# One order over two pairs of steps for each block of nine output products

## The chip, the cores and the metric

The kernel runs on one core of a Trainium2 chip. The metric is device microseconds of one execution. Three runs of the kernel before gave 1625.9, 1626.43 and 1627.45 us; the median, 1626.43, is the time before. The profile is one further execution of 1627.72 us, whose span (first to last instruction of the program) is 1625.8 us.

## The reference

One input `x` (2048 tokens, 512 channels) is normalized and goes through two branches: attention with 32 heads of 16 columns, and an MLP over the token axis (a mixer) with 1792 hidden units.

```python
xn = _layernorm(x)
q, k, v = split_heads(xn @ wqkv)                       # 32 heads of 16
p = softmax(einsum("bhqd,bhkd->bhqk", q, k) * 16**-0.5)
s = merge_heads(einsum("bhqk,bhkd->bhqd", p, v)) @ wo
h = _layernorm(xn)
u = gelu(einsum("bsd,sf->bdf", h, w1) + b1)
y = einsum("bdf,fs->bds", u, w2) + b2
out = x + s * silu(transpose(y))
```

## The kernel before, in words

Heads are worked on two at a time (NP = 16 pairs of heads). For a pair of heads the 2048 x 2048 scores are computed twice: once to find the largest score of each query, and once more, with that maximum subtracted by two extra rows of the operands, for the exponentials. The work is cut into 512 steps, NT = NU = 512, 32 for each pair of heads.

- `max_of` (line 523) issues one matmul into a bank of the ring `ps_mx` (three PSUM banks; line 532) and a VectorE reduction of that bank (line 536). Below, a **maximum** (m).
- `score` (line 980) issues one matmul into a bank of the ring `ps_sc` (four banks; line 987) and a ScalarE exponential that reads it (line 992). Below, a **score** (s). Scores run 22 steps (LEAD) behind the maxima.
- `values` (line 994) multiplies one step's exponentials with the values (line 1003) on all 128 rows of TensorE, two further steps later.

A maximum or a score needs at most 50 of TensorE's rows, so two matmuls run side by side, one on rows 0 to 63 and one on rows 64 to 127. Such a place for two is called a **slot** here. Products of the rest of the network fill the places that the attention leaves free: each of their matmuls over 128 rows is cut into two halves over 64 rows (`halves`, line 1132; the matmul is line 1144). These halves are the letter **D**. First comes the mixer (`mixer`, line 573), then the product with `wo` (`rest`, line 1011): a block of 128 tokens takes nine products, three for each of the first three groups of eight heads, and fourteen blocks (PARTS) are done this way while the maxima still run (steps below NU).

The products of a block add up in one bank, which `Banks.hold` takes out of the front of the ring `ps_sc` when the block's first product is fetched (line 1034), so that the scores go round on three banks. A ScalarE copy in `part` (line 910) empties the bank, and it goes to the end of the ring.

The main loop (line 1227) goes by pairs of steps, s and s+1. A pair has eight maxima, eight scores, two `values` and some D. How many D is set by `count` (line 1155): a block of nine is given out as 4 and 5. The order inside a pair is written out by hand:

```python
4: ("DDDDssmmsmms", "smsmmmssDDDD", 4, 7),
5: ("DDDDDsmsmsmsm", "smsmsmsmDDDDD", 5, 8),
```

The two strings are the two row halves, one letter a slot. The two numbers are places: ahead of the slot with that number stand `values` of one step and `run_later`, and at the first of the two places also `piece`. The half that begins with D changes from pair to pair (`lead`). `values` uses all the rows, so it parts the slots into groups. For a block of nine (a pair with 4 and one with 5) these are: a **three-slot group** (slots 4 to 6 of the first pair), a **ten-slot group** (slots 7 to 11 and the next pair's 0 to 4; nine D), a three-slot group (slots 5 to 7), and a **nine-slot group** (slots 8 to 12 and the next block's first four; nine D, of two blocks).

Other engines' work is issued at those places:

- `run_later` (line 514) runs functions put off with `after(n, f)`, n places later: the copy of the values' sum (`put_away`, line 716), ScalarE's casts of the divided attention (`parts`, line 792, instruction on line 798), the mixer's last identity (line 703, issued at the end of a mixer block) and tanh (line 704), GpSimd's additions, stores.
- `piece` (line 1220) issues one short VectorE job: the two parts of `max_rows` (line 538), once for 16 steps (first a reduction on line 551 and one 32x32 transpose on line 548; later three transposes, GpSimd's cast and subtraction, and four DMAs that put the maxima into the operand rows), or a reciprocal (line 751).
- At the start of each pair the loop calls `divisions` and `load_second`, which issue loads on SP.

Of the kernel before, what the change touches and what calls it, by code (L numbers as in the profile page):

```python
# [21 lines left out]
def tile_attention_token_mixer(ctx, tc, x, wqkv, wo, w1, b1, w2, b2, out):  # L22
    nc = tc.nc
    P = 128
    S, D = x.shape
# [11 lines left out]
    LEAD = 22  # L37
# [132 lines left out]
    with (  # L170
# [97 lines left out]
        def first(c, some=range(4), power=False):  # L268
            def dst(b):
                xn[4 * c + b] = px.tile([P, D], F32, name="xn", bufs=8)  # L270
                return xn[4 * c + b]

            return Norm(lambda b: xr[4 * c + b], dst, some=some, power=power)
# [69 lines left out]
        two = first(0, range(2, 4), True)  # L343
# [64 lines left out]
        for c in range(NC):  # L408
# [20 lines left out]
            for n, (part, g) in enumerate(order):  # L429
                m = slice(g * P, (g + 1) * P)  # L430
# [75 lines left out]
    now = [0]  # L506

    def after(n, f):

        later.append(f if n == 1 else lambda: after(n - 1, f))  # L510
# [3 lines left out]
    def run_later():  # L514
        now, later[:] = soon + later, []
        soon.clear()
        for f in now:
            f()

    NU = NP * NB * 2  # L520
# [406 lines left out]
    def load_second():  # L927

        b = next((b for b in unkept if b >= PARTS), min(unkept))
        unkept.remove(b)  # L930
        i = b - NB // 2
        while not held or len(held) < NB // 8:
            held.append(big.tile([P, S], F32, name="big"))
        ys[b] = held[i // 4][:, i % 4 * 512 : i % 4 * 512 + 512]
        nc.sync.dma_start(ys[b], y_d[b] if b < PARTS else xv[:, b, :])
# [58 lines left out]
    def values(t):  # L994
        p, r = divmod(t, SPP)
        span, kb = divmod(r, NB)
        if kb == 0:
            state["av"] = ps_av.tile([P, 512], F32, name="av")
        av = state["av"]
        for a in range(2):  # L1000
            for c in range(2):
                j = 2 * a + c
                nc.tensor.matmul(  # L1003
                    av[32 * j : 32 * j + 32, :],
                    vps[p][:, kb, 16 * a : 16 * a + 32], prob.pop((t, a, c)),
                    start=kb == 0, stop=kb == NB - 1,
                )
        if kb == NB - 1:
            soon.append(lambda: put_away(p, span, av))
# [46 lines left out]
    class Fill:  # L1056
# [10 lines left out]
        def next(self):  # L1067
            x = self.peek()
            self.ahead.clear()
            return x  # L1070
# [3 lines left out]
    done = 0  # L1074
    n_fill = NF * 3 * NB + NB * 3 * NF
    total = NT + LEAD
# [4 lines left out]
    def take(n, each):  # L1081

        nonlocal open_, done
        got = 0
        while open_ and (got < n or fill.peek() and len(fill.peek()) == 2):
            x = fill.next()
            if x is False:
                open_ = False
            elif x is None:
                break  # L1090
            elif len(x) == 2:
                def then(empty, back):
                    empty()
                    back()

                each(None, lambda x=x: then(*x))
                if fill.peek() is None:
                    fill.next()
                    break
            else:  # L1100
                each(x, None)
                got += 1
        done += got
# [28 lines left out]
    def halves(lead, n):  # L1132


        parts, then = ([], []), []

        def each(x, f):
            if f:
                then.append(f)
                return  # L1140
            ps, w, m, first, last = x
            for a, made in ((lead, parts[0]), (1 - lead, parts[1])):
                r = slice(64 * a, 64 * a + 64)
                made.append(lambda r=r, start=first and a == lead, stop=last and a != lead: nc.tensor.matmul(  # L1144
                    ps, w(r), m(r), start=start, stop=stop,
                ))

        take(n, each)
        return *parts, then
# [3 lines left out]
    new_block = [False]  # L1153

    def count():


        left = -done
        for i, n in enumerate(sizes):
            left += n  # L1160
            if left > 0:
                break
        new_block[0] = left == n
        if left == 9:
            return 4
        return min(6, -(-left // -(-3 * left // (15 if i == SLOW else 16)))) if left > 0 else 0
# [35 lines left out]
    def items(s, a):  # L1202

        mx, sc = [], []
        for i in range(4):
            t = s - LEAD + i // 2
            if s < NU:
                mx.append(lambda i=i: max_of(s + i // 2, i % 2, a))
            if 0 <= t < NT:
                sc.append(lambda t=t, i=i, at=(ps_mx, "mx") if a and s >= NU else (ps_sc, "sc"): score(t, i % 2, a, *at))  # L1210
        return mx, sc

    take(FIRST, whole)
    after(5, lambda: load_v(0))
    if NP > 1:
# [4 lines left out]
    def piece():  # L1220
        if pieces:
            pieces.pop(0)()
            return True
        return False

    lead = 0
    for s in range(0, total + 1, 2):
        t = s - LEAD
        now[0] = s
        if s >= NU or t < 0:  # L1230
            run_later()
        if done >= n_fill // 2 + 3 * NF:
            divisions()
        if s >= NU - SPP + LEAD and unkept:
            load_second()
        if s == NU:

            ps_sc.free += ps_mx.free
            ps_mx.free = ps_sc.free
        heads = [items(s, a) for a in range(2)]  # L1240
        if s < NU and t >= 0:
            steady[0] = True
            one, two, then = halves(lead, count())
            made = [dict(D=part, m=heads[a][0], s=heads[a][1]) for part, a in ((one, lead), (two, 1 - lead))]
            first, second, *places = order(len(one), new_block[0])
            if one:
                lead = 1 - lead
            for i, kinds in enumerate((*zip(first, second), "")):
                if i in places:

                    if i == places[0]:
                        piece()
                    now[0] = s + places.index(i)
                    if now[0] >= LEAD + 2:
                        values(now[0] - LEAD - 2)
                    run_later()
                for of, kind in zip(made, kinds):
                    if of[kind]:
                        of[kind].pop(0)()
            for f in then:  # L1260
                f()
        elif s < NU:

            for i in range(4):
                for a in range(2):
                    max_of(s + i // 2, i % 2, a, *first_banks[n_max % 4])
                    n_max += 1
                end = i == 3 and s + 2 == LEAD
                some = []
                take(EARLY[n_max // 2 % len(EARLY)], lambda *x: some.append(x))  # L1270
                for x in some:
                    lanes(*x, stop=end and x is some[-1])
                if end:
                    keep_half()
                if i == 1:
                    now[0] = s + 1
                    run_later()
        else:


            for i in range(2):

                a_half(*(heads[a][1][2 * i : 2 * i + 2] for a in range(2)), i == 0 or s >= NU + 2 * (PARTS - NB // 2))
                if not piece() and asides and s < total - 2:
                    asides.pop(0)()
                for v in range(t - 2, t + i):
                    if (v, 0, 0) in prob:
                        values(v)
                if i == 0:
                    now[0] = s + 1  # L1290
                    run_later()
            if s == NU + 4:
                load_last_w()
            for _ in in_halves[:2]:
                load_half()
            if s == total - 6:
                split_last_w()
        if s < NU and s % 16 == 14:
            pieces[:0] = max_rows(s + 1)
        while t < 0 and piece():  # L1300
            pass
        for v in (t - 2, t - 1):
            if 0 <= v < NT and (v, 0, 0) in prob:
                values(v)
        if 0 <= t < NT:
            p, r = divmod(t, SPP)
            if r == 0 and p + 1 < NP:
                if p > 0:
                    load_qk(p + 1)
                load_v(p + 1)  # L1310
# [23 lines left out]
    one, two, times, lower = asides  # L1334
# [5 lines left out]
    of = ks[NP - 1][:, :1024].rearrange("p (a q) -> p a q", a=2)  # L1340
# [81 lines left out]
```

## Time and profile before

| | before |
|---|---|
| median of three runs | 1626.43 us |
| the profiled execution | 1627.72 us |
| its span | 1625.8 us |
| TensorE matmul (PE) busy | 1618.6 us, 11937 instructions |
| VectorE (DVE) busy | 1421.3 us, 2492 |
| ScalarE (ACT) busy | 1195.8 us, 2312 |
| maxima, reductions on line 536 | 2026, 682 ns each in the record |
| scores, exponentials on line 992 | 2004, 607 ns each |
| products of `wo` during the maxima, line 1144 | 252 half products, 1402.4 to 1556.4 us |

Times in a row are microseconds from the start of the span. A row of the timeline gives the start, the length, the engine, the line, the operation and what it writes and reads; "x8" merges eight instructions that follow each other on that engine, with the length from the first one's start to the last one's end. PEld is the loading of a matmul's weights. In brackets stands the idle time of the engine ahead of the row and what ended it. A matmul's record is longer than the time until the next may start, so starts are compared, not lengths.

### The profile page before, as it was taken

Reading aid. Unit: us, or ns where it says so; the run is one execution under the profiler, and the core shown is the slowest. Engines: PE = TensorE matmul, PEld = TensorE weight load, DVE = VectorE, ACT = ScalarE, POOL = GpSimd, SP = SyncE. Lnnn points to the kernel's source line nnn. Section 1 sums busy time; section 2 is a strip of 40 time slices with the busy share of each in tenths; the row PEclk is TensorE's granted clock in tenths of the full one; section 3 lists DMA queues with packets and bytes.
Section 4 is the critical chain, followed back from the end, with each engine's and each line's share of the span. In section 5 each row is a group of like instructions: output and inputs, shape, how many; then the busy total and the mean of one; then the engine's idle time right before and its main releaser. Section 6 shows DMA issues by size and latency. Waiting matters only on the chain.

```text
span 1625.8 us, 31245 instructions
## 1 busy us (share of the span) xinstructions
PE 1618.6 (100%) x11937; PEld 876.6 (54%) x11937; DVE 1421.3 (87%) x2492; ACT 1195.8 (74%) x2312; POOL 559.9 (34%) x665
## 2 busy tenths in 40 slices
PE   9999999999999999999999999999999999999998
PEld 7888854554555544544545545545545445444444
DVE  7665999999999999999999999999999999999956
ACT  3333477777777777778877877777777778888885
POOL 1224844342244432342333332322322233632440
PEclk9999999999999999999999999999999999999999
DMA  7478441514142141926151512314151615353365
GB/s 228 177 249 206 114 93 41 95 43 73 41 71 71 32 79 34 244 66 109 39 86 38 86 61 44 76 25 69 38 85 38 112 39 94 120 98 119 115 186 194
DMA packets 152466, 155.60 MB, mean 96 GB/s; under 512 B 51628, under 2 KB 110252, under 8 KB 149244
## 3 DMA queue, kind: packets, MB, share of 16 engines
q1 hardware_dynamic: 147900, 152.85, 38.6%
q8 instruction: 94, 1.54, 0.4%
q0 software_dynamic: 4416, 0.75, 0.4%
q14 instruction: 56, 0.46, 0.1%
HBM read 101.86 MB, written 50.58 MB: 94 GB/s over the span
## 4 chain that ended last, share of the span: by engine, by line
PE 99%; DMA 0%; DVE 0%; ACT 0%; SPq 0%; issue 0%; POOL 0%; DVEq 0%
PE av L1003 31%; PE dn L1144 24%; PE sc L987 16%; PE mx L532 15%; PE sc L435 3%; PE dn L670 3%; PE mx L435 2%; PE av L435 1%; PE sc L101 0%; PE sc L103 0%; PE sc L102 0%; PE mx L987 0%; DMA wl<-in_A_wqkv_dram 0%; PE mx L101 0%; PE mx L103 0%; PE mx L102 0%
## 5 line engine op out<-in xcount | busy, mean ns | idle before, releaser
L536 DVE TENSOR_REDUCE mxp<-mx 128x1 f32<-128x512 f32 x2026 | 1251.8, 682 | 118.3 <-PE mx L532 100.3
L992 ACT ACTIVATE prob<-sc 128x512 f32<-128x512 f32 x2004 | 1039.3, 607 | 284.6 <-PE mx L532 126.8
L532 PE MATMUL mx<-big 48*128 48x512 f32 x2026 | 773.7, 419 | 0.0
L987 PE MATMUL sc<-big 50*128 50x512 f32 x2004 | 739.8, 412 | 0.1
L1003 PE MATMUL av<-prob,vp 128*32 128x512 f32 x4096 | 545.5, 604 | 0.2 <-DVE ev L721 0.2
L1144 PE MATMUL dn<-hu,wh 64*128 64x512 f32 x1520 | 507.4, 404 | 0.0
L987 PEld LDWEIGHTS sc<-big 50*128 50x128 f32 x2004 | 354.2, 186 | 238.8 <-ACT prob L992 210.6
L532 PEld LDWEIGHTS mx<-big 48*128 48x128 f32 x2026 | 358.0, 185 | 195.4 <-DVE mxp L536 178.2
L1144 PEld LDWEIGHTS dn<-hu,wh 64*128 64x128 f32 x1520 | 271.9, 184 | 73.6 <-issue 49.5
L1144 PE MATMUL dn<-hu,wl 64*128 64x512 f32 x762 | 302.3, 397 | 0.0
L1003 PEld LDWEIGHTS av<-prob,vp 128*32 128x32 f32 x4096 | 80.9, 108 | 180.3 <-issue 168.0
L94 POOL TENSOR_TENSOR wl<-raw,wh 128x512 fp32r<-128x512 f32 x124 | 150.7, 1217 | 60.0 <-ACT wh L166 26.6
L1144 PEld LDWEIGHTS dn<-hu,wl 64*128 64x128 f32 x762 | 140.5, 184 | 12.1
L164 POOL CAST wh<-raw 128x512 fp32r<-128x512 f32 x104 | 60.4, 580 | 192.1 <-PE mx L532 79.5
L559 POOL CAST m<-f 16x128 fp32r<-16x128 f32 x32 | 9.0, 280 | 303.6 <-DVE f L548 303.6
L98 POOL DMA_DIRECT2D big<-m x128 | 66.2, 525 | 2.7 <-PE mx L987 2.7
L620 POOL TENSOR_TENSOR sq<-u 128x512 f32<-128x512 f32 x11 | 11.4, 1041 | 133.0 <-ACT u L614 132.9
L1144 PE MATMUL dn<-wh,hu 64*128 64x512 f32 x168 | 55.1, 393 | 0.0
L707 POOL TENSOR_SCALAR t<-t 128x512 f32<-128x512 f32 x16 | 23.8, 1488 | 83.7 <-ACT t L704 83.7
L435 PE MATMUL sc<-xt,big 128*128 128x512 f32 x184 | 44.3, 389 | 0.0
L94 POOL TENSOR_TENSOR hu<-hx,hu 128x512 fp32r<-128x512 f32 x16 | 20.4, 1292 | 68.4 <-ACT hu L278 68.4
L670 PE MATMUL dn<-hu,wh 64*128 64x512 f32 x128 | 42.3, 392 | 0.0
(233 smaller groups left out, 1212.1 us busy)
## 6 DMA issues: line engine op xcount, KB each, us to landing
raw<-in_B_w_dram SPq DMA_DIRECT2D x104, 256.0 KB
big<-k_d SPq DMA_DIRECT2D x96, 128.0 KB
big<-q_d SPq DMA_DIRECT2D x96, 128.0 KB
q_d<-sg SPq DMA_DIRECT2D x16, 512.0 KB
k_d<-sg SPq DMA_DIRECT2D x16, 512.0 KB
num_d<-ev SPq DMA_DIRECT2D x30, 256.0 KB
u_d<-uo SPq DMA_DIRECT2D x14, 512.0 KB
hu<-u_d SPq DMA_DIRECT2D x14, 512.0 KB
```

What stands on the lines that cost most here:

```text
L94: eng.tensor_tensor(out=o, in0=a, in1=b.bitcast(F32), op=OP.subtract)
L98: queue.dma_start(dst.bitcast(F32), src.bitcast(F32))
L164: nc.gpsimd.tensor_copy(whs[n][:, :m, :], raws[n][:, :m, :])
L435: nc.tensor.matmul(ps, w[part][:, kd, m], xt[kd][:, z, :], start=w is wh and z == 0 and kd == 0, stop=w is wl and kd == ND - 1,)
L532: nc.tensor.matmul(ps, q[o : o + 48, r * P : (r + 1) * P], k[o : o + 48, c * 512 : (c + 1) * 512], start=True, stop=True,)
L536: nc.vector.tensor_reduce(mxp[u // 16][:, a, r % 8, c : c + 1], ps, axis=AX.X, op=OP.max)
L670: nc.tensor.matmul(ps, w(slice(0, 64)), m(slice(0, 64)), start=first, stop=last)
L707: nc.gpsimd.tensor_scalar(t, t, 1.0, None, op0=OP.add)
L987: nc.tensor.matmul(ps, ks[p][o : o + 50, kb * P : (kb + 1) * P], qs[p][o : o + 50, at : at + 512], start=True, stop=True,)
L992: nc.scalar.activation(e, ps, AF.Exp, scale=scale)
L1003: nc.tensor.matmul(av[32 * j : 32 * j + 32, :], vps[p][:, kb, 16 * a : 16 * a + 32], prob.pop((t, a, c)), start=kb == 0, stop=kb == NB - 1,)
L1144: made.append(lambda r=r, start=first and a == lead, stop=last and a != lead: nc.tensor.matmul(ps, w(r), m(r), start=start, stop=stop,))
```

## The change: one order of 25 slots for a block

While the blocks of nine run, the loop takes two pairs of steps together. `both_pairs` has an order of 25 slots, with `values` and `run_later` ahead of slots 2, 12, 15 and 24. The nine D of the first half stand in slots 3 to 11, those of the other half in slots 15 to 23. The nine products are fetched, and with them the bank, at slot 3; the copy that empties it is issued behind slot 23. `piece` is called ahead of slots 2 and 15. The groups between `values` are now: slots 2 to 11 (ten slots), 12 to 14 (three), 15 to 23 (nine) and 24 with the next block's 0 and 1 (three). `divisions` and `load_second` of the second pair are called ahead of slot 15. The order is used where s divides by 4, the mixer is done, and a new block of nine is due; the second pair is then passed over.

```diff
+    WIDE = ("mssDDDDDDDDDsmsmsmmssmsmm", "smmsmsmsmsmsmmsDDDDDDDDDs", 2, 12, 15, 24)
+
+    def both_pairs(s, keep):
+
+        heads = [[x + y for x, y in zip(items(s, a), items(s + 2, a))] for a in (lead, 1 - lead)]
+        made = [dict(m=mx, s=sc) for mx, sc in heads]
+        first, second, *places = WIDE
+        one, two, then = [], [], []
+        for i, kinds in enumerate((*zip(first, second), "")):
+            if i in places:
+                n = places.index(i)
+                if n == 2:
+                    keep(s + 2)
+                if n % 2 == 0:
+                    piece()
+                now[0] = s + n
+                values(now[0] - LEAD - 2)
+                run_later()
+            if "D" in kinds and not one and not two:
+                one, two, then = halves(lead, 9)
+                assert len(one) == len(two) == 9
+            for of, rows, kind in zip(made, (one, two), kinds):
+                (rows if kind == "D" else of[kind]).pop(0)()
+            if then and not two:
+                then.pop()()
...
     lead = 0
-    for s in range(0, total + 1, 2):
-        t = s - LEAD
-        now[0] = s
-        if s >= NU or t < 0:
-            run_later()
+    second_pair = None
+
+    def keep(s):
+
         if done >= n_fill // 2 + 3 * NF:
             divisions()
         if s >= NU - SPP + LEAD and unkept:
             load_second()
+
+    for s in range(0, total + 1, 2):
+        t = s - LEAD
+        now[0] = max(s, now[0])
+        if s >= NU or t < 0:
+            run_later()
+        if s != second_pair:
+            keep(s)
...
         heads = [items(s, a) for a in range(2)]
-        if s < NU and t >= 0:
+        if s == second_pair:
+            pass
+        elif s < NU - 2 and s % 4 == 0 and done >= n_fill and count() == 4 and new_block[0]:
+            both_pairs(s, keep)
+            second_pair = s + 2
+        elif s < NU and t >= 0:
```

## The prediction

> **What bounds the kernel now.** First the page: the span, each engine's share of it, the granted clock, and the chain that ended last.
>
> ```profile
> span 1625.8 us, 31245 instructions
> ...
> PE 1618.6 (100%) x11937; PEld 876.6 (54%) x11937; DVE 1421.3 (87%) x2492; ACT 1195.8 (74%) x2312; POOL 559.9 (34%) x665
> ...
> PEclk9999999999999999999999999999999999999999
> ...
> PE 99%; DMA 0%; DVE 0%; ACT 0%; SPq 0%; issue 0%; POOL 0%; DVEq 0%
> ```
>
> TensorE sets the end at full clock, so only time taken from or put onto its stream counts. A busy TensorE may still be waiting (a blocked matmul isn't shown as idle), so second I look for the place: the lines of the changed stage, from the view by source line.
>
> ```profile
> L1144 PE MATMUL dn<-wh,hu x168: 383/391/490, 1402.4 to 1556.4; 64*128 64x512 f32 x168
> L910 ACT COPY t<-dn x14: 592/593/595, 1414.2 to 1557.1; 128x512 f32<-128x512 f32 x14
> ```
>
> The D products of the output blocks run from 1402.4 to 1556.4, up to the last pair of steps with maxima (s=510). Fourteen blocks of two pairs are 56 steps, so the first has s=456: it divides by 4, and the new branch takes all fourteen. One block lasts (1557.1-1414.2)/13 = 10.99 us.
>
> Third, what a block would last unhindered, from the timeline of the mixer, where a pair has 5 D:
>
> ```profile
> 1304.40 1.07 PE L1003 MATMUL av<-prob,vp 128*32 128x512 f32 x8
> ...
> 1305.40 0.49 PE L987 MATMUL sc<-big 50*128 50x512 f32 x1
> ...
> 1306.30 1.07 PE L1003 MATMUL av<-prob,vp 128*32 128x512 f32 x8
> ...
> 1309.85 1.06 PE L1003 MATMUL av<-prob,vp 128*32 128x512 f32 x8
> ```
>
> A pair of 13 slots takes 5.45 us. `values` with its changeover takes 1.00 (1304.40 to the slot at 1305.40), the three-slot group 0.90, the ten-slot group 3.55-1.00 = 2.55. So a slot costs (2.55-0.90)/7, about 0.23. A block has 25 slots, one fewer than two such pairs: 2 x 5.45 - 0.23 = 10.67. The stage loses 0.32 us per block. Where? The timeline of a nine-slot group:
>
> ```profile
> 1456.45 0.49 PE L532 MATMUL mx<-big 48*128 48x512 f32 x1
> ...
> 1456.78 0.40 PE L987 MATMUL sc<-big 50*128 50x512 f32 x1
> ...
> 1457.21 1.09 ACT L992 ACTIVATE prob<-sc 128x512 f32<-128x512 f32 x2 [0.56 <-PE dn L1144]
> ...
> 1457.87 0.18 PEld L987 LDWEIGHTS sc<-big 50*128 50x128 f32 x1 [0.19 <-ACT prob L992]
> ...
> 1458.18 0.59 ACT L910 COPY t<-dn 128x512 f32<-128x512 f32 x1
> ...
> 1458.20 0.40 PE L532 MATMUL mx<-big 48*128 48x512 f32 x1
> ...
> 1459.01 1.07 PE L1003 MATMUL av<-prob,vp 128*32 128x512 f32 x8
> ```
>
> It lasts 2.56 us against 2.55-0.23 = 2.32. The new block has just taken a bank out of the ring, so the score at 1457.87 must use the bank of the score at 1456.78, two scores back: its exponential runs 1457.21 to 1457.81, and the bank is free 0.06 later. The wait is 0.15 (due 1457.72, after the five slots' 0.33 + 4 x 0.23), and the next slot comes 0.33 after instead of 0.23. From here on slot k of a group (from 0) is due at 0.33 + 0.23 x (k-1), `values` 0.37 after the last; an exponential or a reduction starts 0.43 after its matmul, as at 1456.78, and 0.54 after the first of a group, which lasts 0.10 longer. The ten-slot group keeps its own small slip:
>
> ```profile
> 1461.89 0.49 PE L532 MATMUL mx<-big 48*128 48x512 f32 x1
> ...
> 1464.52 1.06 PE L1003 MATMUL av<-prob,vp 128*32 128x512 f32 x8
> ```
>
> 2.63 instead of 2.55: six scores, each on the bank of three scores before, at 0.49 per exponential (1.09 for two, less the second's 0.60). Nothing else is late: 0.24 + 0.08 is the block's 0.32.
>
> **The change, part by part.** Slots, `values` and D are as many as before, and a block still has groups of 10, 3, 9 and 3. What moves is where the bank is taken and emptied, and where `run_later` and `piece` put other engines' work.
>
> *(a) The nine-slot group.* The bank is held from slot 3 to slot 23. Slots 15 to 23 have scores at 16, 19, 20 and 22, each on a bank whose exponential is over before (for slot 20, that of slot 14: it ends 2.1 us after its group's start, 0.2 after the next one's, and slot 20 comes at 1.25). The stall goes: 0.24 per block, in the 13 blocks between first and last, **-3.1 us**. The copy L910 now waits for slot 23, behind the last exponential and in the time of `values`; behind it on ScalarE stand the next group's three exponentials, due after it ends, and without that cover they would come up to 0.59 later, which four banks allow. The ten-slot group has the same six scores with the hold behind the second, and keeps its 0.08. At worst the old stall stays (0), at best that slip goes too (-4.2).
>
> *(b) The two ends.* The groups at which the stage begins and ends:
>
> ```profile
> 1401.15 0.49 PE L532 MATMUL mx<-big 48*128 48x512 f32 x1
> ...
> 1402.42 0.39 PE L1144 MATMUL dn<-wh,hu 64*128 64x512 f32 x1
> 1402.94 0.49 PE L987 MATMUL sc<-big 50*128 50x512 f32 x1
> ...
> 1404.09 0.64 PE L1003 MATMUL av<-prob,vp 128*32 128x512 f32 x4
> ```
>
> ```profile
> 1555.32 0.50 PE L532 MATMUL mx<-big 48*128 48x512 f32 x1
> ...
> 1558.36 0.64 PE L1003 MATMUL av<-prob,vp 128*32 128x512 f32 x4
> ```
>
> The last has ten slots and 3.04 against 2.55: its waits go with the earlier release, **-0.5**. The first has 2.94 against 2.32, stall 0.62. What ScalarE does there:
>
> ```profile
> 1402.29 1.09 ACT L992 ACTIVATE prob<-sc 128x512 f32<-128x512 f32 x2
> 1403.26 0.70 ACT L703 ACTIVATE ev<-dn,b2h 128x512 f32<-128x512 f32 x1
> 1403.83 1.10 ACT L992 ACTIVATE prob<-sc 128x512 f32<-128x512 f32 x2
> 1404.78 0.66 ACT L798 CAST hu<-sq 128x512 fp32r<-128x512 f32 x1
> 1405.29 0.68 ACT L704 ACTIVATE t<-ev 128x512 f32<-128x512 f32 x1
> 1405.82 1.60 ACT L992 ACTIVATE prob<-sc 128x512 f32<-128x512 f32 x3
> ```
>
> After the change two slots stand in place of the four: the second score is due at 1402.66 and waits for the exponential that ends at 1402.89: 0.29, and 0.10 to restart. So 0.39 for 0.62, **-0.2**. But the first `run_later` issues the cast L798 and the tanh L704, and it now stands ahead of the ten-slot group, not of a three-slot one. That group starts at 1402.95+0.37+1.00 = 1404.32; its first exponential could run at 1404.86, but ScalarE reaches it at 1405.82. The fourth score, due 1.25 into the group, needs that bank, free at 1405.82+0.66: a wait of 0.92, and 0.10 to restart, less the usual 0.08: **+0.9**. Bounds: 0 to 1.1, the length of the two instructions with a restart. The later casts L798 change places likewise, from ahead of a ten-slot group (two, some 0.05 each) and to ahead of one (one, 0.2): **+0.1**.
>
> *(c) The pieces on VectorE.* `piece` ran ahead of a three-slot group; now at slots 2 and 15, behind one and ahead of a long group.
>
> ```profile
> 1426.42 0.68 DVE L536 TENSOR_REDUCE mxp<-mx 128x1 f32<-128x512 f32 x1
> 1427.13 0.22 DVE L551 TENSOR_REDUCE neg<-mxp 128x16 f32<-128x64 f32 x1
> 1427.46 0.20 DVE L548 STREAM_TRANSPOSE f<-neg 32x32 f32<-32x32 f32 x1
> 1427.62 4.93 DVE L536 TENSOR_REDUCE mxp<-mx 128x1 f32<-128x512 f32 x8
> 1432.58 0.63 DVE L548 STREAM_TRANSPOSE f<-neg 32x32 f32<-32x32 f32 x3
> 1433.15 1.26 DVE L536 TENSOR_REDUCE mxp<-mx 128x1 f32<-128x512 f32 x2
> ```
>
> Reductions come in chains of eight, 4.93 us or 0.61 a step: three of a three-slot group and five of the long one. Between chains VectorE has about 0.5 us free, and there the pieces lie now, at no cost. Inside the chain there is under 0.1 free. Three transposes (0.57 to the next reduction) put the long group's first reduction from 0.55 to 1.13 after the group's start; its bank is free at 1.13+0.69+0.06 = 1.88. There are three banks for maxima, so the fourth maximum of the group (seventh slot, due at 1.48) waits 0.40 with all of TensorE's stream behind it, restarts for 0.10, and the fifth waits 0.04: 0.54. The pair L551, L548 (0.49 to the next) costs 0.42 in the same way, a reciprocal, below, 0.50.
>
> ```profile
> L751 DVE RECIPROCAL d<-d x2: 549/549/549, 1498.6 to 1542.5; 96x64 f32<-96x64 f32 x2
> ```
>
> Two reciprocals, and as twelve DMAs below, four a set, show, three sets: 3 x (0.42+0.54) + 2 x 0.50 = **+3.9**. No row shows such a wait in mid-group, so the bounds are 0 (the ring absorbs it) and the whole shift with its restart, 0.7 to 0.8 each, 5.9 in all. I take 3.9, since the bank arithmetic is that which gives 2.56 for the nine-slot group.
>
> These rows show VectorE taking pieces in program order between two reductions. The Trainium skill ("PSUM — Partial Sum Buffer", Engine vs sequencer instructions) says that VectorE's queue is strictly first in, first out. By it the reductions can't pass a piece, and the sum stays +1.1; could they, it would be -2.8.
>
> The maxima then reach POOL some 2.4 us later, for a cast, a subtraction and four DMAs:
>
> ```profile
> L98 POOL DMA_DIRECT2D big<-m x12: 502/507/579, 1434.0 to 1523.5; - x12
> ...
> DMA to landing us min/median/max: 1.6/1.6/3.4
> ```
>
> They are read in the ten-slot group of the next block, some 7 us on: 4 x 0.5 of issues and a landing fit, so no cost; a set that lands late by the spread costs 1.8. `keep(s + 2)` issues SP's loads under one group from where they were; they are read blocks later.
>
> **Sum.** -3.1 - 0.5 - 0.2 + 0.9 + 0.1 + 3.9 = +1.1 us. On the profiled execution (1627.72: span 1625.8 and 1.9 around it) 1628.8; on the median of the runs, 1626.43, **1627.5**. A measurement of this kernel can tell about 0.2%, 3.3 us, from no change: this is no change.
>
> **Rivals.**
> - *The pieces and ScalarE's two instructions cost nothing*, because the rings of banks soak them up. Then -3.1-0.5-0.2+0.1 = -3.7: **1622.7**, faster by 0.23%. For it: VectorE is idle for about 1 us of each block (10.7 less 16 x 0.61). Against: that time lies ahead of the three-slot groups, and the pieces are no longer there. Chance 0.15.
> - *The maxima become the bound of every long group.* The fifth maximum (slots 10 and 23) is due at 1.94 and needs the second maximum's bank, free at about 1.90 (0.54+0.61+0.69+0.06). If reductions run 0.06 later than I reckon, each of 27 long groups waits 0.06 and restarts for 0.10: +4.3, in all +5.4, **1631.8**, slower by 0.33%. It passes 0.2% from 0.08 a group on. Against: the old ten-slot group has its maxima nearly as close and loses only 0.08. Chance 0.22.
> - *The order does not do what it says*: a score still meets the taken bank two scores back, or the branch isn't entered; then about **1626.4**. The banks above and s=456 speak against it. Chance 0.05.
>
> My forecast has 0.58. The first rival counts as faster, with a little of the forecast's tail; the second as slower: faster 0.15, same 0.62, slower 0.23. The range of 1622.5 to 1632 takes in the bounds of (c) and both rivals' times.
>
> **What would show it.** In the profile after: copies L910 about 10.7 us apart in blocks without a piece and 11.2 to 11.7 in those with; nine-slot groups of 2.32; L548, L551 and L751 inside a chain of reductions, with the fourth maximum behind them late by 0.3 to 0.4; the first block about a microsecond longer than the next. Blocks with pieces as short as the others prove the first rival, long groups of 2.7 everywhere the second.

## The result and the profile after

The changed kernel takes **1628.72 us** (median of 22 runs, 1627.34 to 1629.86); the kernel before, in 22 runs beside it, 1625.98 (1625.02 to 1627.45). The ratio is 1.0016, 95% interval 1.001 to 1.0023: 2.7 us more, against a forecast of 1.1 more. The interval leaves out 1, so the loss is small but real. Its profiled execution took 1628.28 us. First the page of the kernel after: TensorE is as busy as before at the full clock, and the chain that ended last still runs along it, but now DMAs have 1% of it, where before they had 0%.

```profile
span 1626.4 us, 31244 instructions
...
PE 1616.9 (99%) x11937; PEld 875.9 (54%) x11937; DVE 1421.5 (87%) x2492; ACT 1197.8 (74%) x2312; POOL 561.2 (35%) x665
...
PEclk9999999999999999999999999999999999999999
...
PE 96%; DVE 1%; DMA 1%; ACT 0%; POOL 0%; issue 0%; SPq 0%; DVEq 0%; POOLq 0%
```

Next the view by source line, kernel after (count, ns min/median/max, first and last start).

```profile
L1144 PE MATMUL dn<-wh,hu x168: 383/393/501, 1402.4 to 1553.6; 64*128 64x512 f32 x168
...
L910 ACT COPY t<-dn x14: 579/604/604, 1411.4 to 1554.6; 128x512 f32<-128x512 f32 x14
```

A block lasts (1554.6-1411.4)/13 = 11.02 us, against 10.99 before: on average nothing is won. That mean hides two effects of nearly the same size. The timeline of the kernel after shows them. First a nine-slot group with no piece ahead of it:

```profile
1452.39 0.50 PE L532 MATMUL mx<-big 48*128 48x512 f32 x1
...
1453.44 0.39 PE L987 MATMUL sc<-big 50*128 50x512 f32 x1
1453.67 0.39 PE L987 MATMUL sc<-big 50*128 50x512 f32 x1
...
1454.70 1.07 PE L1003 MATMUL av<-prob,vp 128*32 128x512 f32 x8
1455.31 0.60 ACT L910 COPY t<-dn 128x512 f32<-128x512 f32 x1
```

It lasts 2.31 us, where it lasted 2.56: the third score follows the second after one slot's 0.23, and waits no more. L910 lies under `values`. Then a nine-slot group with three transposes ahead of its reductions:

```profile
1430.40 0.50 PE L532 MATMUL mx<-big 48*128 48x512 f32 x1
...
1431.00 0.63 DVE L548 STREAM_TRANSPOSE f<-neg 32x32 f32<-32x32 f32 x3
...
1431.56 3.03 DVE L536 TENSOR_REDUCE mxp<-mx 128x1 f32<-128x512 f32 x5
...
1432.25 0.18 PEld L532 LDWEIGHTS mx<-big 48*128 48x128 f32 x1 [0.61 <-DVE mxp L536]
1432.25 0.50 PE L532 MATMUL mx<-big 48*128 48x512 f32 x1 [0.17 <-DVE mxp L536]
...
1432.85 0.50 PE L532 MATMUL mx<-big 48*128 48x512 f32 x1
...
1433.28 1.06 PE L1003 MATMUL av<-prob,vp 128*32 128x512 f32 x8
```

It lasts 2.88. The first reduction starts 1.16 after the group (forecast 1.13), so the fourth maximum, due at 1431.88, starts at 1432.25, and the brackets name VectorE as what it waited for. The wait is 0.37 (forecast 0.40); the fifth comes 0.60 behind it, where 0.46 for two slots and 0.10 for the restart make 0.56: the forecast's further 0.04. The first block's ten-slot group, same kernel and view:

```profile
1402.11 0.49 PE L987 MATMUL sc<-big 50*128 50x512 f32 x1
...
1402.45 0.65 ACT L798 CAST hu<-sq 128x512 fp32r<-128x512 f32 x1
...
1402.96 0.68 ACT L704 ACTIVATE t<-ev 128x512 f32<-128x512 f32 x1
...
1403.49 3.07 ACT L992 ACTIVATE prob<-sc 128x512 f32<-128x512 f32 x6
...
1404.17 0.50 PE L987 MATMUL sc<-big 50*128 50x512 f32 x1 [0.41 <-ACT prob L992]
...
1405.57 1.06 PE L1003 MATMUL av<-prob,vp 128*32 128x512 f32 x8
```

3.46 us against the usual 2.63: the fourth score stands behind an exponential that stands behind the cast and the tanh. So far the forecast's steps hold. The end of the stage does not follow it. The view of the chain that ended last, kernel after (start, length, what):

```profile
1541.07 0.56 DVE d L751
1541.64 0.32 SPq L752
1542.01 0.43 SPq L921
...
1544.17 9.09 DMA uo<-rec_d
...
1553.39 1.28 POOL u L786
1554.68 1.23 POOL sq L786
1555.91 0.55 POOL hu L798
1556.56 1.30 POOL hu L94
1557.89 0.50 PE dn L1188
...
1565.91 0.55 POOL big L98
1566.46 3.98 DMA big<-m
```

Read downwards, this is the last group of heads: its reciprocal, the store and the load that spreads it over the rows, and GpSimd's in-order work behind the load, until the D product can start. The timeline of the same stretch shows what TensorE loses:

```profile
1554.93 0.49 PE L532 MATMUL mx<-big 48*128 48x512 f32 x1
...
1556.52 0.49 PE L1188 MATMUL dn<-wh,hu 64*128 64x512 f32 x1 [0.63 <-POOL hu L798]
...
1557.89 0.50 PE L1188 MATMUL dn<-wh,hu 64*128 64x512 f32 x1 [0.65 <-POOL hu L94]
...
1558.33 1.92 PE L1003 MATMUL av<-prob,vp 128*32 128x512 f32 x16
...
1570.57 0.46 PE L987 MATMUL sc<-big 50*128 50x512 f32 x1 [0.63 <-DMA big<-m]
```

The last group, now six slots, lasts 3.40 us, where 0.33 + 4 x 0.23 + 0.37 = 1.62 were due: a wait of 1.78. Later a score waits another 0.7 for the last set of maxima (L98), which GpSimd sends behind all that. In the kernel before, the same load kept GpSimd waiting 3.5 us, not 6.6 (timeline, before: the reciprocal, the use of the load, the first D of the last heads):

```profile
1542.49 0.55 DVE L751 RECIPROCAL d<-d 96x64 f32<-96x64 f32 x1
...
1552.90 1.28 POOL L786 TENSOR_TENSOR u<-u,uo 96x512 f32<-96x512 f32 x1 [3.49 <-DMA uo<-rec_d]
...
1557.56 0.40 PE L1188 MATMUL dn<-wh,hu 64*128 64x512 f32 x1
```

To compare the two I count from the start of the stage's first group, 1401.15 before and 1398.82 after. This D ran 156.4 us on before and is due 156.9 us on after (0.8 into the last group), so it isn't wanted earlier. What moved is the load: its use comes 151.8 us on before and 154.6 on after, 2.8 later. Of these, 0.9 are the reciprocal, 0.5 the store L921 that SP now issues ahead of the load, and 1.4 that the load takes 9.2 us from issue to use instead of 7.8.

**Where the time went**, in us, from the starts of the groups in both profiles:

| step | forecast | measured |
|---|---|---|
| 13 nine-slot groups, 2.57 to 2.31 | -3.1 | -3.4 |
| ten-slot groups, 2.63 to 2.60 on average | 0 | -0.3 |
| first group, wait of 0.62 to 0.43 | -0.2 | -0.2 |
| first block's ten-slot group, 2.63 to 3.46 | +0.9 | +0.8 |
| a later cast L798 (ten-slot group of 2.77) | +0.1 | +0.1 |
| eight pieces: 3 x 0.57, 2 x 0.45, and 0.35 + 0.66 + 0.25 | +3.9 | +3.9 |
| last group, wait of 0.50 to 1.78 | -0.5 | +1.3 |
| wait for the last maxima, 0 to 0.1, now 0.7 | 0 | +0.6 |
| sum | +1.1 | +2.8 |

### The profile page after: what moved, and what is told of

Same layout as the page of the kernel before. It is cut to its first block, busy times and chain, and to the rows that moved or that the text cites. A ratio compares the mean times of both kernels' runs of the same rounds, so it can differ in the third digit from the quotient of the medians.

```text
span 1626.4 us, 31244 instructions
## 1 busy us (share of the span) xinstructions
PE 1616.9 (99%) x11937; PEld 875.9 (54%) x11937; DVE 1421.5 (87%) x2492; ACT 1197.8 (74%) x2312; POOL 561.2 (35%) x665
## 4 chain that ended last, share of the span: by engine, by line
PE 96%; DVE 1%; DMA 1%; ACT 0%; POOL 0%; issue 0%; SPq 0%; DVEq 0%; POOLq 0%
PE av L1003 30%; PE dn L1144 23%; PE sc L987 16%; PE mx L532 14%; PE sc L435 3%; PE mx L435 2%; PE dn L670 2%; DVE mxp L536 1%; PE av L435 1%; PE dn L671 1%; DMA uo<-rec_d 1%; PE sc L101 0%; PE sc L103 0%; PE sc L102 0%; PE mx L339 0%; PE dn L1188 0%
## 5 line engine op out<-in xcount | busy, mean ns | idle before, releaser
L94 POOL TENSOR_TENSOR wl<-raw,wh 128x512 fp32r<-128x512 f32 x124 | 150.8, 1218 | 60.4 <-ACT wh L166 27.2
L98 POOL DMA_DIRECT2D big<-m x128 | 66.4, 527 | 2.7 <-PE mx L987 2.7
L1144 PE MATMUL dn<-wh,hu 64*128 64x512 f32 x168 | 60.9, 410 | 0.0
L94 POOL TENSOR_TENSOR hu<-hx,hu 128x512 fp32r<-128x512 f32 x16 | 20.4, 1294 | 68.5 <-ACT hu L278 68.5
```

The lines of the kernel that those rows point to most:

```text
L94: eng.tensor_tensor(out=o, in0=a, in1=b.bitcast(F32), op=OP.subtract)
L98: queue.dma_start(dst.bitcast(F32), src.bitcast(F32))
```

## The experiments

My theory: the gain in the groups and the pieces' price are as forecast, and what I missed is the load of the last reciprocals with GpSimd's queue behind it (the kernel before has the same chain, with room to spare). The rival: the stage isn't what sets the end, or the groups' gain isn't real.

**A second profile of the kernel before.** Its first profile reaches the first nine-slot group at 1401.15 us, the kernel after at 1398.82. Is that the change?

> The kernel before, unchanged, for a second profile. Between the two profiles read so far the changed kernel is 2.3 us slower from the first nine-slot group on, yet reaches that group 2.3 us earlier. Theory: the first profile of before lost that time ahead of the stage by chance, so this one reaches its first nine-slot group near 1399 (first profile 1401.15) and has the same lengths inside the stage: nine-slot groups 2.57, ten-slot groups 2.63, last group 3.0 to 3.1. Rival: the change itself makes the part ahead of the stage faster; then 1401 again.

It took 1626.14 us and reached that group at 1399.58, with all groups of the stage as long as in the first profile of before. So the difference ahead of the stage lies within the spread of single executions: over all the profiles of this document, five with the old order reach that group between 1399.58 and 1401.15, eight with the new order between 1398.82 and 1401.16. I compare stretches within the stage: from there to the first group with the transposes L828, before_again takes 1399.58 to 1572.71 = 173.13, the kernel after 1398.82 to 1574.84 = 176.02, 2.9 more.

**The pieces alone, in the old order.** If the pieces' place has the price I gave, it shows without the new order:

```diff
-                    if i == places[0]:
+                    if i == places[done > n_fill]:
                         piece()
```

> The kernel before with one part of the change alone: in the stage of the output blocks the VectorE pieces are called at the second place of a pair (behind a three-slot group, ahead of a long one) instead of the first. Theory (a piece inside the chain of eight reductions makes the long group wait for a bank of a maximum): ten-slot groups behind L551 and its transpose longer by 0.4, nine-slot groups behind three transposes or a reciprocal by about 0.2 only, because the wait for the exponential there runs beside it; in all 3 x 0.65 + 2 x 0.2 = 2.3 us slower than before. Rival (the three banks soak it up): no group longer, 0 us.

1631.57 against 1626.29 us, ratio 1.0035 (1.0021 to 1.0049): 5.3 more. The groups cost what was expected, 2.3 in all: ten-slot groups behind L551 and L548 at 3.00, 3.01 and 2.88, nine-slot groups behind transposes at 2.86 and behind a reciprocal at 2.75 and 2.76. But 3.0 came on top: the last group lasted 4.90 instead of 3.05, and what follows it came later again. The last reciprocal is a piece too; it ran at 1545.52 and its load arrived at 1556.08, 145.9 and 156.4 us from the start of the stage's first group, where before_again has 141.3 and 151.8. The place of the pieces has a second price, off VectorE.

**Without the wait for that load.** The last division multiplies the numerators by themselves, which needs no load, in both kernels; so they leave out the division for the last six heads in half of the tokens:

```diff
-    eng().tensor_tensor(out=num[c][rows, :], in0=num[c][rows, :], in1=rec[rows, c, :], op=OP.mult)
+    by = num[c][rows, :] if (g, span) == (ND - 1, QH - 1) else rec[rows, c, :]
+    eng().tensor_tensor(out=num[c][rows, :], in0=num[c][rows, :], in1=by, op=OP.mult)
```

> The kernel before, where the last division (heads 24 to 29, second half of the queries) multiplies the numerators by themselves instead of by the loaded reciprocals, so that those outputs are wrong and GpSimd does the same work without waiting for the load. Theory (at the end of the stage the first products of the last group of heads wait for GpSimd, which waits for this load): before waited little for it, last group 2.8 to 3.05 instead of 3.05, time 0 to 0.5 us less than before. Rival (that wait is ScalarE's and the banks'): no change either, so this one only sets the mark for its twin with the new order.

> The changed kernel with the same edit (the last division multiplies by the numerators instead of the loaded reciprocals; those outputs are wrong). Theory: the six-slot last group falls from 3.40 to 1.6 to 1.8, the wait of 0.7 for the maxima's landing near 1570 goes, and the time falls by 2.0 to 2.5 us against the changed kernel, to 0.2 to 0.7 over before (1626.2 to 1626.7 beside 1626.0). Rival (the last group waits for ScalarE or for banks): it stays 3.2 to 3.4 and the time stays 2.5 to 2.9 over before.

Before: 1626.05 against 1626.29, ratio 0.9998 (0.999 to 1.0007), the last group 3.05 as it was. So the 0.50 that the last group lost in the old order is not the load's. After: 1626.98, ratio 1.0005 (0.9996 to 1.0014); the last group falls from 3.40 to 1.87 and the wait near 1570 is gone. These are 1.5 + 0.7 of the 2.8. By the traces the load costs the kernel before nothing and the kernel after 2.2 us (by the medians, each against the kernel before beside it, 2.0): theory held. The 0.7 that is left over the kernel before is about the 2.8 less 2.2, though its interval doesn't tell it from nothing.

**The pieces put under cover.** In the new order, slot 2 is ahead of a ten-slot group and slot 15 of a nine-slot one; slot 12 is ahead of a three-slot group. So the second piece goes to slot 12, and to give the load time the last reciprocals are issued one place earlier:

```diff
-                if n % 2 == 0:
+                if n < 2:
                     piece()
...
-        after(8 if g < ND - 1 else 2, lambda: pieces.append(two))
+        after(8 if g < ND - 1 else 1, lambda: pieces.append(two))
```

> The changed kernel with the VectorE pieces called at the places with n below 2, that is ahead of slots 2 and 12 instead of 2 and 15, and the reciprocal of the last group of heads put off by one place less, so that it too falls on slot 12. Theory: the three transposes and the two reciprocals now lie in VectorE's idle time ahead of a three-slot group, so the five nine-slot groups of 2.75 to 2.88 fall to 2.31 (2.6 us); L551 and its transpose ahead of slot 2 still cost 0.3 to 0.7 a set; and the load of reciprocals is issued 1.9 us earlier, so that the last group falls from 3.40 to about 2. In all 4 us less than the changed kernel: 1.5 to 2 us less than before. Rival (where a piece stands does not matter, the changed kernel loses through the order itself): nine-slot groups stay as they are, time within 1 us of the changed kernel.

1629.03 against 1627.48 us, ratio 1.0008 (0.9999 to 1.0017). The groups are right: 2.30 to 2.32 in all nine-slot groups but the last, also where transposes or a reciprocal run. At the end the gain is given back: GpSimd now waits 13.5 us for the load, one nine-slot group has 2.70, the last group 2.15, and a score waits about 3.0 us for the last maxima. The second half of my expectation fell.

**And the first block in the old order** (`done > n_fill` instead of `>=`), so that the cast and the tanh lie ahead of a three-slot group again:

> The same, and the first of the fourteen blocks keeps the old order of two pairs. Theory: ScalarE's cast and the mixer's last tanh stand ahead of a three-slot group again, so the ten-slot group of 3.47 there is 2.62 while the group ahead of it keeps its 2.93: 0.6 to 0.7 us less than the run beside it, 2.1 to 2.7 us less than before. Rival (the 3.47 comes from the start of the new order, whichever block starts it): the second block shows it instead, no gain.

1629.34, ratio 1.0012 (1.0003 to 1.0021). The ten-slot group of 3.45 in the run beside it is 2.63, as it was before the change, so those two ScalarE instructions were its cause; the end again takes all. (The profiled execution, 1627.64 us, is the fastest of this kernel's eleven; what the slower ones lose besides, no trace shows.) The timeline of this kernel says how (GpSimd, and the score that waits):

```profile
1548.63 1.28 POOL L786 TENSOR_TENSOR u<-u,uo 96x512 f32<-96x512 f32 x1 [13.14 <-DMA big<-y_d]
...
1551.12 1.29 POOL L913 TENSOR_TENSOR t<-t,gt 128x512 f32<-128x512 f32 x1
1552.49 1.29 POOL L914 TENSOR_TENSOR t<-t,xt 128x512 f32<-128x512 f32 x1
...
1556.78 1.30 POOL L94 TENSOR_TENSOR hu<-sq,hu 96x512 fp32r<-96x512 f32 x1
...
1561.75 0.75 POOL L559 CAST m<-f 16x128 fp32r<-16x128 f32 x1
...
1569.85 0.46 PE L987 MATMUL sc<-big 50*128 50x512 f32 x1 [2.06 <-DMA big<-m]
```

The load arrives at 1548.63, in the kernel after at 1553.39, but `times` (L786) is now issued ahead of the two additions L913 and L914 of the thirteenth block. They were done during the wait; now they stand behind it, 2.6 us of work, and from 1548.63 to 1562.5 GpSimd isn't free. A second thing moved with them: the kernel gives the subtraction `sub` (L94) to GpSimd in steps below NU and to VectorE from there on. The second half's subtraction (`hu<-sq,hu`) ran on VectorE in the kernel after, at 1556.62; issued one place earlier it is GpSimd's, 1.3 us more. (The releaser in the first bracket is the transfer that ended last by the profile; the instruction reads what rec_d brings.)

**Clearing the unused rows ahead of the wait.** This took the memset and the second multiplication out of GpSimd's chain between the load and the first D; the multiplication was put back behind the first half's subtraction:

```diff
+        if late:
+            for c in range(2):
+                made.append(hu.tile([P, 2, 512], F32R, name="hu"))
+                nc.gpsimd.memset(made[c][DH * n :, :, :].bitcast(F32), 0.0)
...
-            for c in range(2):
+            for c in range(1 if late else 2):
```

> The same as the run beside it, and in the last division GpSimd clears the unused rows ahead of its wait for the load instead of behind, and treats the first 512 columns whole (multiply, cast, subtract) ahead of the others' multiplication. Theory: GpSimd's chain from the load to the first product is 1.2 us shorter and to the last maxima 1.8 shorter, which takes what is left of the waits at the end: 0 to 0.7 us less than the run beside it. Rival (nothing is left to wait for there): the same within 0.3 us.

1632.87, ratio 1.0031 (1.002 to 1.0041). The expectation of a gain fell. The timeline of this kernel, ScalarE and the weights of a score:

```profile
1556.19 0.62 ACT L804 CAST hu<-sq 96x512 fp32r<-96x512 f32 x1 [5.11 <-POOL sq L807]
...
1557.36 0.28 PEld L993 LDWEIGHTS sc<-big 50*128 50x128 f32 x1 [5.00 <-ACT prob L998]
```

ScalarE's cast waited 5.11 us for the multiplication that I had put back, with the exponentials behind it in ScalarE's queue, and so TensorE stood 5.00: a nine-slot group of 7.63. The Trainium skill ("Perfetto Trace Analysis", Tensor Engine Instruction) says that ScalarE, VectorE and GpSimd are strictly first in, first out; these 5 us agree.

**Four runs on the end alone**, three on the covered kernel with the first block in the old order, one on the kernel before. The first takes the load's wait away as above; the second issues `times` two places later, so that L913 and L914 stand ahead of it again; the third and fourth cast and subtract the last set of maxima on VectorE and store it from SP:

```diff
-        after(8 if now[0] < NU - 16 else 2, times)
+        after(8 if now[0] < NU - 16 else 4, times)
...
+            on, queue = (nc.vector, nc.sync) if u >= NU - 2 else (nc.gpsimd, nc.gpsimd)
-            nc.gpsimd.tensor_copy(m[:, 0, :], f[:16, :])
+            on.tensor_copy(m[:, 0, :], f[:16, :])
```

> The kernel after, with the pieces at slots 2 and 12 (ahead of a ten-slot and of a three-slot group), the first block in the old order and the reciprocals of the last group of heads issued one place earlier, and besides with the last division multiplying the numerators by themselves instead of by the loaded reciprocals, so that GpSimd waits for no load there (the last 6 heads of half of the tokens get other values). Theory (what such an order gains in the stage is eaten behind it, by GpSimd's queue that stands behind the load): the groups stay as without the edit (nine-slot 2.31, ten-slot behind the first reduction and transpose 2.84 to 3.28), the last group falls from 2.17 to 1.9 or less and the wait of 2.1 us near 1566 goes, so about 3 us less than before, ratio 0.9980 to 0.9988. Rival (the stage's gain is not real): the ratio stays at 1.000 or over.

> The kernel after, with the pieces at slots 2 and 12, the first block in the old order and the last reciprocals one place earlier, and the multiplications by the loaded reciprocals issued two places later, so that GpSimd's two additions of the thirteenth block stand ahead of the wait for the load, not behind it. Theory (the wait near 1566 comes from work that the load holds up in GpSimd's queue): GpSimd reaches the cast of the last maxima 1 to 2.5 us earlier, that wait falls from 2.1 to under 1 us, ratio to before 0.9985 to 0.9995. Rival (it is the load's arrival itself, with the chain of multiplications and subtractions behind it): nothing changes, ratio 1.001.

> The kernel after, with the pieces at slots 2 and 12, the first block in the old order and the last reciprocals one place earlier, and with the last set of maxima cast and subtracted on VectorE and stored from SP's queue, instead of GpSimd. Theory (those maxima are late because their cast stands behind GpSimd's wait for the load): the cast comes at 1557 instead of 1562, and if SP issues the four stores by 1562 they land ahead of the scores near 1566; the wait of 2.1 us there goes, ratio to before 0.9992 to 1.0000 (1.0012 without the edit). Rival: SP's own queue, which stands for 5 us behind a wait in that stretch, holds the stores up as long: no change, ratio 1.001.

> The kernel before, with the last set of maxima cast and subtracted on VectorE and stored from SP's queue. It has the same wait for that set near 1568, 0.65 to 0.8 us. Theory: the wait goes, 0.6 us less, ratio 0.9996; rival: SP's queue is no earlier, ratio 1.000 or over.

Beside a kernel before of 1626.25 us (33 runs):

| run | us | ratio | last group | wait near 1566 |
|---|---|---|---|---|
| covered_no_load_wait | 1623.93 | 0.9985 (0.9976 to 0.9993) | 1.88 | none |
| covered_turn | 1623.88 | 0.9986 (0.9977 to 0.9994) | 1.87 | none |
| covered_last_set_vector | 1625.01 | 0.9992 (0.9983 to 1.0001) | 2.15 | none |
| before_last_set_vector | 1626.20 | 0.9999 (0.999 to 1.0008) | 3.04 | none |

The first shows that the groups' gain is real once nothing waits for the load. The second is as fast and computes all of it: **2.4 us under the kernel before**, and by the two ratios 0.3% under the kernel after. Its timeline:

```profile
1540.85 0.69 SPq L779 DMA_DIRECT2D uo<-rec_d  x1
...
1542.92 1.28 POOL L913 TENSOR_TENSOR t<-t,gt 128x512 f32<-128x512 f32 x1 [8.07 <-ACT t L910]
...
1548.39 1.28 POOL L786 TENSOR_TENSOR u<-u,uo 96x512 f32<-96x512 f32 x1 [2.83 <-DMA uo<-rec_d]
...
1554.12 0.39 PE L1188 MATMUL dn<-wh,hu 64*128 64x512 f32 x1
...
1555.01 1.65 DVE L94 TENSOR_TENSOR hu<-sq,hu 96x512 fp32r<-96x512 f32 x1 [0.48 <-ACT hu L798]
...
1557.75 0.28 POOL L559 CAST m<-f 16x128 fp32r<-16x128 f32 x1
```

GpSimd does the additions while the load is on its way, waits 2.83 instead of 13.14, and reaches the cast of the maxima at 1557.75 instead of 1561.75 (of which 0.7 is that the stage began earlier). From the load's arrival to that cast it takes 9.4 us instead of 13.1: 2.6 less for the two additions and 1.3 less for the second subtraction, which is VectorE's again. So this run changed two things, and which of them would have done alone wasn't tried. The third loses the wait near 1566 as expected, but a nine-slot group lasts 3.05, as ScalarE's cast waits 1.00 for the multiplication, which the load still holds up. The fourth won nothing: in the kernel before there is almost no such wait to take (0 to 0.1 us by the starts of the groups; the 0.65 to 0.8 that I expected do not show in them).

## Why the prediction was right, and where it was not

The forecast was no change, 1627.5 us, and the result lies 1.2 above it, within the range. But 22 runs tell more finely than the 0.2% that the forecast allowed them: the kernel after is slower by 0.16%. That "no change" stood is in part luck. The end of the stage cost 2.4 us more than forecast, the groups 0.7 less, and the difference of 1.7 is small beside the 3.3 us that I called no change. By its steps:

- **(a) the nine-slot group.** Right, by its cause too: 2.31 against 2.32 forecast. The term was 0.3 us too small over the 13 groups: 0.26 a group (2.57 on average to 2.31) and not 0.24. The ten-slot slip stayed, but for 0.03 a group.
- **(b) the first group and block.** Right in size: 0.43 of wait for 0.39, +0.8 for +0.9. That the cast and the tanh are the cause is shown by after_covered_first, where the group is 2.63 with the two ahead of a three-slot group.
- **(b) the last group.** This step failed: "its waits go with the earlier release, -0.5" measured +1.3. The old wait did shrink, by about half: without the load's wait the group lasts 1.87 where 1.62 were due, so 0.25 of the 0.50 is left. But it was no longer the last thing to come: the last heads' D stand from 0.8 us into the group on, and the load behind their reciprocal, 2.8 us later in the stage than before, had not come. I had not followed that chain at all. The reciprocal as a piece, its store and load on SP, and GpSimd's in-order chain were named in no step; I said of SP's loads only that "they are read blocks later", which holds for all but the last. after_no_load_wait (-2.2 us of waits) shows it for both places where it is paid.
- **(c) the pieces.** Right, 3.9 for 3.9, with the fourth maximum as the one that waits. The rule weighed there (the Trainium skill, "PSUM — Partial Sum Buffer", Engine vs sequencer instructions) agrees: no reduction passed the transposes, the next one starts at 1431.56 behind them. In parts, transposes cost 0.57 (forecast 0.54) and reciprocals 0.45 (0.50), but L551 with L548 between 0.25 and 0.66 (0.42 forecast, 0.42 on average). That the price belongs to the place is shown by after_covered, where the nine-slot groups lose it, and before_pieces_late, where the old order gains it. In that step the maxima's way over GpSimd was held to cost nothing. That is so for three sets of four; for the last, behind the load, a score waits 0.6 us more than before.
- **The rivals.** The first, that pieces and ScalarE's instructions cost nothing, is refuted by 2.88 and 3.46. The second, that maxima bound every long group, by 2.31 and 2.58 to 2.65 in groups without pieces; that the measured 2.7 us lies between my 1.1 and its 5.4 says nothing for it. The third is refuted by 2.31.

Open: why the load in the kernel after took 9.2 us from its issue to its use, where it took 7.8 and 7.9 in the two profiles of the kernel before, 7.5 in covered_turn and 6.6 in after_covered_first. In the kernel after a store of a block (L921) is issued on the same queue 2.2 us ahead of it, in the other four 1.2 behind it; that this is the cause wasn't tried.

## What to carry to other kernels

Where an order is rewritten, write down for each engine what stands under cover at the old places, and look for cover of the same kind in the new order: here a piece of 0.5 us is free ahead of three reductions and costs about its full shift ahead of five. Follow the last use of each moved job to the end of the stage: a job that has a block of slack within the stage has none behind the last block. Here a load that came earlier helped only once GpSimd's queue held less behind the wait for it. So look at what stands behind such a wait, and at which engine a moved job lands on; put work that needs no load ahead of the wait.

## What the runs showed that I had not expected

GpSimd stands still for 2.7 us ahead of the DMAs of the last set, in every kernel (timeline of the kernel after, an earlier set and the last):

```profile
1432.46 2.08 POOL L98 DMA_DIRECT2D big<-m  x4
...
1565.91 2.05 POOL L98 DMA_DIRECT2D big<-m  x4 [2.69 <-PE mx L987]
```

The releaser in the bracket changes from kernel to kernel (a score, a D product, "issue"), but the length is 2.69 to 2.71 in all eleven profiles that have this row; where the last set goes over VectorE and SP, GpSimd's next DMA (L879 in the kernel before, one line lower there) has a pause of 3.2 instead. So it belongs to GpSimd's first DMA at that point of the program and not to what the bracket names; what it is stays open. The landing of those small stores also takes 4.0 us there, against the median of 1.6 that the prediction's row shows for all of them.
